# One slot of the K matmuls moved ahead of the last convolution chunk of the first bundle

## The chip, the cores and the metric

The kernel runs on one core of a Trainium2 chip. The metric is the device time of one execution in microseconds; the median over runs is compared. Engines are named as in the profile: PE multiplies matrices (PEld loads its weights), DVE and ACT work element by element, POOL and SP mostly issue DMAs. Each engine takes its own instructions in the order in which the program gives them, and waits on semaphores for the others.

## What is computed

The input x has 8 batches of 4160 rows and 192 columns. A causal convolution of 7 taps comes first; its taps are a softmax of `weight`, one set for each of 8 heads of 24 columns. Its output, called y here, goes into a channel mix:

```python
x_prev = np.concatenate([np.zeros((B, 1, D)), x[:, :-1, :]], axis=1)   # x is y, the convolution's output
xk = mu_k * x + (1.0 - mu_k) * x_prev
xr = mu_r * x + (1.0 - mu_r) * x_prev
k = np.maximum(xk @ w_k, 0.0)          # 192 -> 1024
v = k * k @ w_v                        # 1024 -> 192
r = 1.0 / (1.0 + np.exp(-(xr @ w_r)))  # 192 -> 192
return r * v
```

The kernel multiplies in bf16 and adds up in fp32.

## The kernel before

**Tiling.** Batches go in pairs; the two batches of a pair lie in the two halves of the 128 partitions, and the 192 columns in three chunks of 64 (`NC` = 3). y is kept transposed (`yT`, columns on partitions, time along the row). Time is cut into steps of 512 rows; the first step and two others have 256. A step of L rows has L*8/512 slots: a slot is one PSUM tile of 128 by 1024 fp32 that holds a part of the K product (`k_mm`, L592), read by one ReLU on ACT (`k_relu`, L604) and squared by one DVE instruction (`k_square`, L618). The first step has slots 0 to 3, the second 4 to 11. Four slots make a bundle, and the bundles are run in order; the last loop of the file calls one function for each.

**A first-step slot.** `k_mm` of a slot of the first step issues 12 matmuls of 64 by 256: three column chunks, two blocks of 128 output columns, and the two halves of the partitions, which alternate. So the first matmul of a slot reads the weights `wk` in partitions 0 to 63 and the second those in partitions 64 to 127.

**The order is written by hand.** The whole program is emitted under a manual schedule: each engine gets its instructions in the order of the calls. PSUM tiles come from a ring of four, given out in turn, so a tile is reused by the fourth allocation after it, once its readers are done.

**Before the bundles.** `prologue()` issues the loads. K's weights are loaded in four DMAs by POOL (`load_wk`, L225): output columns 0 to 511 for partitions 0 to 63, the same for 64 to 127, then columns 512 to 1023 likewise. Slots 0 and 1 need the first two, slots 2 and 3 the others. PE runs matmuls on zeros in the meantime.

**Bundle one** (`bundle_first`) makes y for the first two groups of rows (3 and 4 blocks of 120 rows) straight in transposed form. There are six chunks, one for each group and each 64 columns. `conv_t` (L412) issues 24 matmuls for a chunk of the first group and 32 for one of the second, and `to_yT` (L422) copies the result from PSUM to `yT` on ACT. For the first group DVE then forms the difference of neighbours (`diff`, L535) and xk (`mix`, L548). After the loop, DVE forms the second step's difference and xk, the first column chunk ahead and the other two later (`diff`, L535; `scale`, L566; `add_y`, L572): `diff(1, slice(1, 3))` needs the copies of the fifth and sixth chunk. PE goes on with slots 0 to 3. The four squares are at the end of the bundle, after the second step's xk in DVE's order.

**Bundle two** (`bundle_second`) has slots 4 to 7, which read the second step's xk, between the three chunks of the third group. The first two of these are copied by DVE (L422), the third by ACT. Bundles three and four use `bundle_third` and `bundle_rest`; there PE also transposes y of a group (`tr`, L501, copied by DVE at L510), and convolves later groups in another form (L318, L392). A one-element memset on DVE (`x_tile`, L124) stands ahead of the x loads of each later group, and POOL's load waits for it.

Of the kernel before, what the change touches and what calls it, by code (L numbers as in the profile page):

```python
# [14 lines left out]
def kernel(  # L15
# [47 lines left out]
    for p in range(NPAIR):  # L63
# [5 lines left out]
        for L in sizes:  # L69
            ns = L * NF // STEP  # L70
# [8 lines left out]
    n = 0  # L79
# [102 lines left out]
    n = groups[0][2] * 2 * D  # L182
# [97 lines left out]
    def turn_mu():  # L280
        nc.tensor.transpose(out=warm_ps[:, 1, 0 : 2 * NC], in_=mu_raw, identity=ident6)
# [120 lines left out]
    def conv_t(g, c, o, blocks):  # L402

        for n, i in enumerate(blocks):
            for first_piece in (True, False):
                for s in range(2):
                    for q in range(2):
                        c0 = c * Q + q * 32
                        lo, hi = c0 // G, (c0 + 31) // G
                        h, m = (hi, 32) if first_piece else (lo, hi * G - c0)  # L410
                        p0 = s * Q + q * 32
                        nc.tensor.matmul(  # L412
                            out=o[p0 : p0 + m, n * BLK : (n + 1) * BLK],
                            lhsT=xbs[g][:, i, s, c0 : c0 + m],
                            rhs=toe[:, h, 0:BLK],
                            start=True,
                            stop=True,
                        )

    def to_yT(g, c, o, b0, b1, copy):  # L420
        c0 = YC + groups[g][1] + b0 * BLK
        copy(out=yTs[0][:, c, c0 : c0 + (b1 - b0) * BLK], in_=o[:, 0 : (b1 - b0) * BLK])  # L422
# [28 lines left out]
    def new_yT(p):  # L451
        yTs[p] = two.tile([P, 3, -(-(YC + S) // 16) * 16], BF16, tag="yT", name="yT")
        y_drams[p] = dram.tile([NROW, 2 * D], BF16, tag=f"y{p % 2}", name="y_dram")
        nc.vector.memset(yTs[p][:, :, 0:YC], 0.0)
# [76 lines left out]
    def diff(s, cs=slice(0, 3)):  # L531
        L = steps[s][2]
        if cs.start == 0:
            diffs[s] = three.tile([P, 3, STEP], BF16, tag="diff", name="d")
        nc.vector.tensor_tensor(  # L535
            out=shaped(s, diffs[s][:, cs, :L]), in0=y_of(s, cs, 1), in1=y_of(s, cs, 0), op=ALU.subtract
        )

    def mix(s, i, sl=slice(0, NC)):

        L = steps[s][2]
        d = diffs[s]
        if s == 0 and i == 0:
            if sl.start == 0:
                xks[s] = two.tile([P, NC, STEP], BF16, tag="xk", name="xk")
            t = xks[s]
            c = sl.start
            nc.vector.scalar_tensor_tensor(  # L548
                out=t[:, c, :L],
                in0=d[:, c, :L],  # L550
                scalar=mu[:, i, c : c + 1],
                in1=y_of(s, sl, 0)[:, 0, :],
                op0=ALU.mult,
                op1=ALU.add,
            )
            return
        scale(s, i, *range(sl.start, sl.stop))
        add_y(s, i, sl)

    def scale(s, i, *cs):  # L560
        L = steps[s][2]
        if s not in (xks, xrs)[i]:
            (xks, xrs)[i][s] = (two, three)[i].tile([P, NC, STEP], BF16, tag=("xk", "xr")[i], name=("xk", "xr")[i])
        t = (xks, xrs)[i][s]
        for c in cs:
            nc.vector.tensor_scalar(  # L566
                out=t[:, c, :L], in0=diffs[s][:, c, :L], scalar1=mu[:, i, c : c + 1], scalar2=None, op0=ALU.mult
            )

    def add_y(s, i, sl=slice(0, NC)):  # L570
        o = shaped(s, (xks, xrs)[i][s][:, sl, : steps[s][2]])
        nc.vector.tensor_tensor(out=o, in0=o, in1=y_of(s, sl, 0), op=ALU.add)  # L572
# [3 lines left out]
    def k_mm(n, cs=range(NC)):  # L576


        s, j = slots[n]
        L = steps[s][2]  # L580
        xk = xks[s]
        if cs[0] == 0 and n not in k_ps:
            k_ps[n] = ring.tile([P, 2, BANK], FP32, tag="k", name="ps_k")
        ps = k_ps[n]
        nf = STEP // L

        for c in cs:
            for f in range(nf):
                fs = slice((j * nf + f) * P, (j * nf + f + 1) * P)
                for i in range(2):  # L590
                    r = slice(i * Q, (i + 1) * Q)
                    nc.tensor.matmul(  # L592
                        out=ps[:, i, f * L : (f + 1) * L],
                        lhsT=wk[r, c, fs],
                        rhs=xk[r, c, :L],
                        start=c == 0 and f == 0,
                        stop=c == NC - 1 and f == nf - 1,
                    )

    def k_relu(n):  # L600
        ps = k_ps.pop(n)
        k_sb = four.tile([P, 2 * STEP], BF16, tag="k_sb", name="k_sb")
        k_sbs[n] = k_sb
        nc.scalar.activation(out=k_sb, in_=ps.rearrange("p a b -> p (a b)"), func=AF.Relu)  # L604

    def k_square(n):
        s, j = slots[n]
        L = steps[s][2]
        k_sb = k_sbs.pop(n)
        if j == 0:  # L610
            k2s[s] = three.tile([P, NF, 2 * STEP], BF16, tag="k2", name="k2")
        nf = STEP // L
        i = k_sb
        o = k2s[s][:, j, :]
        if nf > 1:
            i = k_sb.rearrange("p (b f t) -> p f b t", b=2, f=nf)
            o = k2s[s][:, j * nf : (j + 1) * nf, 0 : 2 * L].rearrange("p f (b t) -> p f b t", b=2)
        nc.vector.tensor_tensor(out=o, in0=i, in1=i, op=ALU.mult)  # L618
# [198 lines left out]
    def run(table, b, part=slice(None)):  # L817
        for fn, a in table.get(b, [])[part]:
            fn(*a)
# [50 lines left out]
    def bundle_first(ns):  # L870
        new_yT(0)
        tiles = [ring.tile([P, 2, BANK], FP32, tag="k", name="ps_t") for _ in range(2)]
        for n, (g, c) in enumerate((g, c) for g in range(2) for c in range(NC)):
            o = tiles[n % 2][:, n // 2 % 2, :]
            conv_t(g, c, o, range(groups[g][2]))
            if n == 0:
                turn_mu()
            to_yT(g, c, o, 0, groups[g][2], nc.scalar.copy)
            if g == 0:
                diff(0, slice(c, c + 1))  # L880
                if c == 0:
                    nc.vector.tensor_copy(out=mu.rearrange("p i c -> p (i c)"), in_=warm_ps[:, 1, 0 : 2 * NC])
                mix(0, 0, slice(c, c + 1))

        diff(1, slice(0, 1))
        mix(1, 0, slice(0, 1))
        for n in ns[:2]:
            k_mm(n)
            k_relu(n)
        diff(1, slice(1, 3))  # L890
        scale(1, 0, 1, 2)
        add_y(1, 0, slice(1, 3))
        for n in ns[2:]:
            k_mm(n)
            k_relu(n)
        for n in ns:
            k_square(n)
        run(late, 0)
# [111 lines left out]
    with tc.manual_schedule():  # L1010
        prologue()
        for b in range(-20, 0):
            for table in (early, rq, rs, xt, mix_a, mix_b, mix_c, vq, late):
                assert b not in table, b
        for b in range(quads[-1][2] + 1):
            run(early, b)
            if b == 0:
                bundle_first(bundles[b])
            elif b == 1:
                bundle_second(b, bundles[b])  # L1020
            elif b == 2:
                bundle_third(b, bundles[b])
            elif b < len(bundles):
                bundle_rest(b, bundles[b])
            else:
                if b == len(bundles):
                    k_square(bundles[-1][3])
                    v_out(*vq[b - 1][0])
                run(rq, b)
                run(rs, b)  # L1030
                for q in vq.get(b, ()):
                    v(*q)
                    v_out(*q)
                run(late, b)
# [30 lines left out]
```

## Time and profile before

| what | us |
|---|---|
| median of 3 runs (411.14 to 412.48) | 412.45 |
| the profiled execution | 411.14 |
| its span, first to last instruction | 409.4 |
| PE busy | 401.5 (98%) |
| DVE busy | 371.3 (91%) |
| ACT busy | 354.6 (87%) |
| mean granted clock of PE | 1.000 |

The span is the time between the first and the last instruction on the core; the rest of the profiled execution's time lies around it. Busy times of different engines overlap. A timeline line gives start and length in us, engine, source line, operation, output and inputs, the shape, how many instructions were merged into the line, and in brackets the idle time before it with the event that ended it. A merged line's length runs from the first start to the last end. Matmuls are pipelined: one starts before the one ahead of it has ended, and their ends are modelled.

### The profile page before, as it was taken

Reading aid. Unit: us, or ns where it says so; the run is one execution under the profiler, and the core shown is the slowest. Engines: PE = TensorE matmul, PEld = TensorE weight load, DVE = VectorE, ACT = ScalarE, POOL = GpSimd, SP = SyncE. Lnnn points to the kernel's source line nnn. Section 1 sums busy time; section 2 is a strip of 40 time slices with the busy share of each in tenths; the row PEclk is TensorE's granted clock in tenths of the full one; section 3 lists DMA queues with packets and bytes.
Section 4 is the critical chain, followed back from the end, with each engine's and each line's share of the span. In section 5 each row is a group of like instructions: output and inputs, shape, how many; then the busy total and the mean of one; then the engine's idle time right before and its main releaser. Section 6 shows DMA issues by size and latency. Waiting matters only on the chain.

```text
span 409.4 us, 17415 instructions
## 1 busy us (share of the span) xinstructions
PE 401.5 (98%) x7670; PEld 303.8 (74%) x7670; DVE 371.3 (91%) x672; ACT 354.6 (87%) x426; POOL 57.7 (14%) x91
## 2 busy tenths in 40 slices
PE   7999999999999999999999999999999999999996
PEld 4667767767867777777877777777777778777795
DVE  5999899998989999989999998999999899999973
ACT  5999988898998889998898998889899878877781
POOL 8622022030060004104020022000000000000000
PEclk9999999999999999999999999999999999999999
DMA  9999989996779988989995998977523756221223
GB/s 148 191 200 202 190 186 215 244 199 189 152 105 221 257 176 125 226 231 169 197 151 152 227 176 123 171 196 187 132 78 90 199 143 159 79 72 48 78 80 117
DMA packets 139123, 66.35 MB, mean 162 GB/s; under 512 B 89364, under 2 KB 139048, under 8 KB 139048
## 3 DMA queue, kind: packets, MB, share of 16 engines
q1 hardware_dynamic: 95704, 48.32, 47.6%
q0 software_dynamic: 42544, 16.36, 34.4%
q8 instruction: 60, 0.98, 1.0%
q10 hardware_dynamic: 800, 0.57, 0.5%
q14 instruction: 15, 0.12, 0.1%
HBM read 33.29 MB, written 36.99 MB: 172 GB/s over the span
## 4 chain that ended last, share of the span: by engine, by line
PE 93%; DMA 3%; DVE 2%; issue 0%; ACT 0%; ACTq 0%; DVEq 0%
PE ps_v L680 41%; PE ps_k L592 39%; PE ps_r L649 8%; PE ps_c L363 2%; DMA xb<-in_x_dram 2%; PE ps_v L632 1%; PE ps_t L412 1%; DMA x_f<-in_x_dram 1%; PE ps_c L318 1%; DVE k L618 1%; DVE yT L422 0%; ACT yT L422 0%; DVE o_sb L696 0%; DVE xk L566 0%; DVE d L535 0%
## 5 line engine op out<-in xcount | busy, mean ns | idle before, releaser
L604 ACT ACTIVATE k_sb<-ps_k 128x1024 bf16<-128x1024 f32 x260 | 253.4, 1040 | 32.9 <-PE ps_k L592 32.2
L618 DVE TENSOR_TENSOR k<-k_sb 128x1024 bf16<-128x1024 bf16 x260 | 173.2, 686 | 24.8 <-ACT k_sb L604 24.5
L592 PE MATMUL ps_k<-xk,wk 64*128 64x512 bf16 (+1 forms) x1632 | 191.7, 367 | 0.8 <-DMA wk<-in_moe_w_k_dram 0.5
L680 PE MATMUL ps_v<-wv,k 64*128 64x192 bf16 x4032 | 188.6, 243 | 0.1
L680 PEld LDWEIGHTS <-k 64*128 64x128 bf16 x4032 | 168.7, 94 | 12.4 <-issue 4.7
L592 PEld LDWEIGHTS <-wk 64*128 64x128 bf16 x1632 | 84.2, 94 | 55.0 <-issue 1.0
L153 POOL DMA_DIRECT2D xb<-in_x_dram x62 | 43.7, 714 | 142.3 <-DVE xb L124 58.1
L696 DVE TENSOR_TENSOR o_sb<-ps_v,r_sb 128x768 f32<-128x768 f32 x64 | 60.8, 949 | 2.6 <-issue 2.4
L660 ACT ACTIVATE r_sb<-ps_r 128x768 bf16<-128x768 f32 x65 | 53.7, 828 | 9.2 <-PE ps_v L680 7.6
L336 ACT CAST y<-ps_c 128x960 bf16<-128x960 f32 (+2 forms) x84 | 52.6, 709 | 0.0
L649 PEld LDWEIGHTS <-xr 64*128 64x128 bf16 x780 | 34.8, 94 | 14.5 <-issue 0.7
L649 PE MATMUL ps_r<-wr,xr 64*128 64x192 bf16 x780 | 43.4, 243 | 0.1
L566 DVE TENSOR_SCALAR xr<-d,mu 128x512 bf16<-128x512 bf16 (+1 forms) x102 | 35.7, 354 | 0.0
L535 DVE TENSOR_TENSOR d<-yT 128x1536 bf16<-128x1536 bf16 (+4 forms) x36 | 31.2, 866 | 2.0 <-ACT yT L422 2.0
L566 DVE TENSOR_SCALAR xk<-d,mu 128x512 bf16<-128x512 bf16 (+1 forms) x99 | 32.8, 360 | 0.1
L572 DVE TENSOR_TENSOR xr<-xr,yT 128x1536 bf16<-128x1536 bf16 (+1 forms) x33 | 31.1, 941 | 1.1
L572 DVE TENSOR_TENSOR xk<-xk,yT 128x1536 bf16<-128x1536 bf16 (+3 forms) x33 | 30.4, 923 | 0.1
L519 POOL COPY y_tail<-yT 128x195 bf16<-128x195 bf16 x4 | 3.1, 774 | 89.7 <-DMA yT<-y_dram 89.7
L363 PEld LDWEIGHTS <-toe 32*32 32x32 bf16 x640 | 4.4, 87 | 8.6 <-issue 7.4
L363 PE MATMUL ps_c<-xb,toe 32*32 32x240 bf16 x640 | 9.3, 267 | 0.0
L126 POOL MEMSET xb<- 32x384 bf16 x3 | 1.2, 408 | 55.5 <-DVE xb L124 48.6
L412 PEld LDWEIGHTS <-xb 128*32 128x32 bf16 (+3 forms) x264 | 5.1, 116 | 3.0 <-ACT xb L246 1.7
(58 smaller groups left out, 65.7 us busy)
## 6 DMA issues: line engine op xcount, KB each, us to landing
out_dram<-o_sb SPq DMA_DIRECT2D x128, 192.0 KB
xb<-in_x_dram POOLq DMA_DIRECT2D x52, 240.0 KB, 8.5
y_dram<-y SPq DMA_DIRECT2D x40, 195.0 KB
y_dram<-y SPq DMA_DIRECT2D x16, 210.0 KB
xb<-in_x_dram POOLq DMA_DIRECT2D x4, 228.0 KB, 5.0
xb<-in_x_dram POOLq DMA_DIRECT2D x4, 192.0 KB, 7.0
wk<-in_moe_w_k_dram POOLq DMA_DIRECT2D x4, 192.0 KB, 6.5
xb<-in_x_dram POOLq DMA_DIRECT2D x2, 216.0 KB, 5.0
```

The source lines that it names most:

```text
L153: nc.gpsimd.dma_start(out=xb[q0 : q0 + rows, lo:hi, s, :], in_=bass.AP(tensor=x.tensor, offset=x.offset + (b * S + t0 + lo * step) * D, ap ...
L336: nc.scalar.copy(out=bass.AP(tensor=y.tensor, offset=y.offset + d, ap=[y.ap[0], [m * 2 * D, 2], [2 * D, m], [Q, 2], [1, b - a]],), in_=bas ...
L535: nc.vector.tensor_tensor(out=shaped(s, diffs[s][:, cs, :L]), in0=y_of(s, cs, 1), in1=y_of(s, cs, 0), op=ALU.subtract)
L566: nc.vector.tensor_scalar(out=t[:, c, :L], in0=diffs[s][:, c, :L], scalar1=mu[:, i, c : c + 1], scalar2=None, op0=ALU.mult)
L572: nc.vector.tensor_tensor(out=o, in0=o, in1=y_of(s, sl, 0), op=ALU.add)
L592: nc.tensor.matmul(out=ps[:, i, f * L : (f + 1) * L], lhsT=wk[r, c, fs], rhs=xk[r, c, :L], start=c == 0 and f == 0, stop=c == NC - 1 and f ...
L604: nc.scalar.activation(out=k_sb, in_=ps.rearrange("p a b -> p (a b)"), func=AF.Relu)
L618: nc.vector.tensor_tensor(out=o, in0=i, in1=i, op=ALU.mult)
L649: nc.tensor.matmul(out=ps[:, i, k * D : (k + 1) * D], lhsT=xr[q, c, ts], rhs=wr[q, c, :], start=c == 0, stop=c == NC - 1,)
L660: nc.scalar.activation(out=r_sbs[s, j], in_=r_ps.pop((s, j))[:, :, 0 : 2 * D], func=AF.Sigmoid)
L680: nc.tensor.matmul(out=v_ps[s, j][:, bank, k * D : (k + 1) * D], lhsT=k2s[s][q, f, t * P : (t + 1) * P], rhs=wv[q, f, :], start=half == 0 ...
L696: nc.vector.tensor_tensor(out=o_sb.rearrange("p (b t) d -> p b (t d)", b=2), in0=v_ps.pop((s, j)), in1=r_sbs.pop((s, j)), op=ALU.mult,)
```

## The change

Slot 0 of the first step (its 12 matmuls and its ReLU) is emitted inside the loop over the six chunks, before the sixth (`n == 5`), in place of after the loop. Slot 1 stays where it was. Nothing else is touched.

```diff
@@ in bundle_first
         for n, (g, c) in enumerate((g, c) for g in range(2) for c in range(NC)):
             o = tiles[n % 2][:, n // 2 % 2, :]
+            if n == 5:
+                k_mm(ns[0])
+                k_relu(ns[0])
             conv_t(g, c, o, range(groups[g][2]))
             if n == 0:
                 turn_mu()
...
         diff(1, slice(0, 1))
         mix(1, 0, slice(0, 1))
-        for n in ns[:2]:
-            k_mm(n)
-            k_relu(n)
+        k_mm(ns[1])
+        k_relu(ns[1])
         diff(1, slice(1, 3))
         scale(1, 0, 1, 2)
         add_y(1, 0, slice(1, 3))
```

On PE the 12 matmuls of slot 0 now stand ahead of the 32 matmuls of the sixth chunk, and on ACT slot 0's ReLU stands ahead of the sixth chunk's copy. The order on DVE, POOL and SP is the same, and so is the order in which PSUM tiles are given out.

## The prediction

> **What bounds the kernel now.** I read the page's busy table first (PE 98% of the span, DVE 91%, ACT 87%), then the table of stretches, to see which engine has no room at which time.
>
> ```profile
> core 0: us, PE busy (x) PEld busy (x) DVE busy (x) ACT busy (x) POOL busy (x), PEclk, DMA share, GB/s
> 16.00:20.30 4.30, 4.07 (x126) 2.63 (x124) 4.26 (x12) 4.15 (x5) 2.80 (x5) 1.00 1.59 192
> 20.30:29.70 9.40, 8.95 (x147) 6.22 (x141) 9.33 (x19) 9.08 (x12) 1.75 (x4) 1.00 1.58 193
> 29.70:45.70 16.00, 15.95 (x290) 11.49 (x291) 15.80 (x28) 15.32 (x21) 4.04 (x6) 1.00 1.12 201
> 45.70:100.00 54.30, 54.30 (x980) 40.22 (x980) 49.74 (x91) 49.27 (x61) 8.85 (x13) 1.00 1.10 214
> 100.00:400.00 300.00, 299.85 (x5749) 229.15 (x5746) 278.59 (x492) 264.26 (x313) 27.27 (x41) 1.00 0.74 150
> ```
>
> From 29.7 us on PE has 0.2 us of idle time in 370 us: a start that is late by x ends late by x. From 16 to 29.7 us it is DVE that has no room (13.59 of 13.70 us busy), while PE has 0.68 us. The edit lies before that, at 10 to 14 us, so the question is what DVE gets there and when. The chain of waits, in order of time, gives it (start, us, what):
>
> ```profile
> 8.91 1.80 PE ps_t L412 x41
> 10.73 1.08 ACT yT L422 x2
> 11.84 0.71 DVE d L535
> 12.57 0.94 DVE xk L566 x2
> 13.53 0.69 DVE xk L572
> 14.22 2.50 DVE k L618 x4
> 16.72 1.13 DVE yT L422 x2
> ```
>
> The last two of bundle one's six convolution chunks are copied by ACT (10.73, 11.25), and the moment the sixth copy ends DVE starts the difference for the second step; from 11.84 on DVE is never free. The chain later passes through a load of x (18.77 to 26.67), but DVE goes on working beside that load, so I follow DVE, not the load. The timelines of PE (first five lines; the last is the place where PE next waits for DVE) and ACT (two lines), then the issue of K's weights and the landing of their second piece (asked for alone):
>
> ```profile
> 7.24 3.96 PE L412 MATMUL ps_t<-toe,xb 128*32 128x120 bf16 x144
> 11.13 1.60 PE L592 MATMUL ps_k<-xk,wk 64*128 64x256 bf16 x25
> 13.19 2.78 PE L592 MATMUL ps_k<-xk,wk 64*128 64x256 bf16 x35 [0.46 <-DMA wk<-in_moe_w_k_dram]
> 17.71 0.60 PE L412 MATMUL ps_t<-toe,xb 128*32 128x120 bf16 x32
> 29.75 0.82 PE L592 MATMUL ps_k<-xk,wk 64*128 64x512 bf16 x6 [0.26 <-DVE yT L510]
> ...
> 10.73 1.07 ACT L422 CAST yT<-ps_t 128x480 bf16<-128x480 f32 x2 [0.24 <-PE ps_t L412]
> 12.11 6.74 ACT L604 ACTIVATE k_sb<-ps_k 128x1024 bf16<-128x1024 f32 x7 [0.30 <-PE ps_k L592]
> ...
> 4.20 2.55 POOL L225 DMA_DIRECT2D wk<-in_moe_w_k_dram x4
> L225 POOL DMA_DIRECT2D wk<-in_moe_w_k_dram x1: 640/640/640, 4.9 to 4.9; - x1
> DMA to landing us min/median/max: 6.3/6.3/6.3
> ```
>
> Two things to see. The second piece of K's first half (rows 64 to 127, needed by every second matmul of slot 0) is issued at 4.9 us and lands 6.3 us later, at 11.2; slot 0's matmuls begin at 11.13. So in the old order the sixth chunk filled PE while these weights were on their way. And ACT's seven ReLUs stand 0.95 us apart ((6.74-1.02)/6, one taking 1.02), the two copies 0.52 apart (one 0.56).
>
> **The change part by part.** Nothing is added or taken away; on PE 12 matmuls and their weight loads (slot 0) pass ahead of the 32 of chunk six, on ACT slot 0's ReLU passes ahead of the copy of chunk six. DVE's, POOL's and SP's orders stay. Slot 0's xk is done on DVE at 10.11 (9.63+0.48) and its output buffer was read last at 8.0, so neither holds it.
>
> 1. PE reaches slot 0 earlier. Chunk five's copy starts at 10.73 after waiting for PE, and a matmul there takes about 0.3 us from start to end, so its last one starts near 10.4. Slot 0's first matmul can run then; the second waits for the weights of 11.2. PE stalls about 0.8 us, and queued behind it are chunk six and slot 1, which need nothing of these weights' second piece or have it later.
> 2. Slot 0 itself then runs as before, from 11.24 for 12 x 0.055 = 0.66 us of issue (25 take 1.60 less the 0.27 tail of the last, so 0.055 each), and its ReLU starts at 12.11 as before. The move brings this ReLU nothing.
> 3. Chunk six follows at about 12.0 and takes 0.60 (the row of 32 such matmuls at 17.71): done at 12.6 instead of 11.2.
> 4. Its copy now stands behind slot 0's ReLU on ACT: it starts one ReLU spacing after 12.11, at 13.06, and ends at 13.62; before, 11.80 (10.73+1.07). That is +1.8. ACT's 0.30 wait before slot 0's ReLU grows to 0.8, since the copy that stood in it is gone.
> 5. DVE's difference of the second step goes from 11.84 to about 13.65. Queued behind it in program order are the scaling and adding (done 14.22, then 16.0), the four squares, the casts of the third group and all of bundles two and three. Nothing of DVE's can pass. The idle time that could take some of it back is 0.03 us from 13.2 to 16 and 0.11 from 16 to 29.7: 0.14.
> 6. On PE the wait of 0.46 for the second half of K's weights goes (PE gets there at about 13.2, where the old wait ended), but slots 4 and 5 now wait for the second step's xk, from about 14.5 to 16.0. This is not a second cost: PE needs DVE again at 29.75, and that wait is the later one.
> 7. DMA: the x loads tied to DVE's tiny memset at 18.39 are issued 1.7 later. Their issue-to-landing of 8 to 9 us is queueing behind other loads, and their users in bundle four run at 39 us against landings to 31: hidden, with 7 us to spare.
>
> Sum: 1.81 - 0.14 = 1.7 us at 29.75 us, and no room after it. The profiled execution took 411.14 (409.4 of span, 1.7 around it): 412.8. It is the shortest of the three shown; on the median of 412.45 the same step gives 414.15.
>
> Bounds of the one unknown, when the weights land: the four pieces' times to landing run from 6.0 to 7.0 us, so 10.9 to 11.9 for this one. With 10.9 the copy would end 0.3 earlier: +1.4. With 11.9 the ReLU would start at 12.8 and the copy end at 14.3: +2.4, of which the old order would itself pay up to 0.6, since there too the ReLUs would run later into squares that have no room. I take 11.2, as measured, and keep +1.4 to +2.4.
>
> **The clock against the row.** PE's matmul rate steps up just at the place of the edit. The same 128x120 matmuls, first from 6.3 to 10.3 us and then from 10.72 to 11.0:
>
> ```profile
> L412 PE MATMUL ps_t<-toe,xb 128*32 128x120 bf16 x68 | 3.9, 302 | 0.8 <-ACT xb L246 0.8
> L412 PE MATMUL ps_t<-toe,xb 128*32 128x120 bf16 x16 | 0.6, 231 | 0.0
> ```
>
> A chunk of 32 took 0.80 to 0.82 us of the timeline before this step (start to start of two copies: 9.93 to 10.73) and 0.60 with its tail after. The profile's granted clock reads 1.00 all through, so it does not show the step; only the durations do. In the sum I take the step where the trace has it. [...]
>
> **The rivals.**
>
> *A, the other side: the fast rate comes late, and it is slower beyond the bound.* If PE goes on at its slow rate through slot 0 and chunk six, slot 0 takes 302/231 to 0.80/0.44 times as long (0.44 is the 0.60 less a tail of about 0.16 hidden under the next matmul), up to 1.2 us instead of 0.66, and the chunk 0.80. The ReLU starts at 12.65, chunk six ends near 13.6, its copy at 14.2: +2.4 to +2.5, and squares behind late ReLUs may add some tenths. That is 414.9 to 415.2. For it: the stall comes at 10.4, the step at about 10.6. Against: PE had idle gaps in the stretch before and stepped up all the same. It decides where the step moves past about 11.2.
>
> *B, the delay is partly taken up.* Two of the three times shown are 1.3 us above the profiled one. If that excess is a wait of DVE's between 11.84 and 29.7 (ReLUs that come later when PE is slow), the new delay eats it first: 1.7 - 1.3 = 0.4, so 412.9; from an excess of 1.7 on, no change at all, 412.45. For it: the squares follow the ReLUs closely (the fourth ReLU ends at 15.99, its square starts at 16.03). Against: the excess may as well lie ahead of the edit, in the first loads, and then it simply adds.
>
> *C, it does what it says and helps.* If K's weights were there by 10.4, slot 0's ReLU would fill ACT right after the copy of chunk five and ACT's 0.30 us wait would go: -0.3, 412.15. But the copy of chunk six would still stand a ReLU later, 0.95 us on DVE, so this needs DVE to have 1 us of room, which the table of stretches excludes; with the weights alone it is +0.95, 413.4.
>
> **How the numbers follow.** The main case (DVE late by about 1.7, all of it kept) has 0.55: 414.1, with 413.6 to 414.7 as its own range. A has 0.27, B 0.14, C 0.04. A measurement of this kernel tells about 0.5%, 2.06 us, from no change; so slower means above 414.51. The main case gives a quarter of itself to that (0.13), A three quarters (0.20): 0.33 slower. Faster, below 410.39, needs a gain that no row offers: 0.03. The rest, 0.64, is within. The range leaves out a tenth on each side: below 412.6 lies the full form of B, above 415.2 the end of A.
>
> **What the new profile should show.** On PE, one or two matmuls of slot 0 near 10.45, a wait of 0.7 to 0.8 us for the DMA of wk, the rest at 11.24, then 32 matmuls of chunk six, and a wait of about 1.5 us at 14.5 that ends with DVE's xk. On ACT, an idle time of 0.8 ahead of the first ReLU (still 12.1), then the copy at 13.06 to 13.62. On DVE, 1.8 us idle before the difference at 13.65, and none up to about 31. PE's wait for DVE's copy of the transposes at about 31.45. I am wrong if DVE shows idle time between 14 and 31 in either kernel's usual run, if the weights land much off 11.2, or if chunk six takes 0.8 instead of 0.6.

## The result and the profile after

The changed kernel takes 413.30 us (median of 22 runs, 411.99 to 415.94) against 412.12 for the kernel before (22 runs, 410.46 to 412.71). The ratio is 1.0040, with a 95% interval from 1.0027 to 1.0053: 1.65 us longer (0.0040 x 412.12), between 1.1 and 2.2. That is inside the 0.5% that the prediction took as its bound for "no change", though clear of zero with this many runs. The means of the same runs, 413.50 and 411.86, lie 1.64 apart; the plain difference of the two medians is only 1.18.

The page's head of the changed kernel; the busy times of DVE and ACT are as before, PE's is 1.4 us higher, and the span is longer:

```profile
span 412.0 us, 17415 instructions
PE 402.9 (98%) x7670; PEld 303.9 (74%) x7670; DVE 371.1 (90%) x672; ACT 354.5 (86%) x426; POOL 57.6 (14%) x91
```

The profiled execution took 413.72, 2.58 more than that of before (411.14). Its chain of waits, in order of time from 8 to 32 us (start, us, what):

```profile
4.88 6.57 DMA wk<-in_moe_w_k_dram
11.45 0.05 issue
11.50 0.84 PE ps_k L592 x11
12.36 1.02 ACT k_sb L604
13.38 0.48 ACT yT L422
13.88 0.70 DVE d L535
...
31.57 0.60 PE ps_k L592 x3
```

Before, this chain came from the convolution chunks through two copies to DVE at 11.84. Now it starts at the second DMA of K's weights (issued 4.88, landed 11.45), goes through slot 0's matmuls and its ReLU, and only then to the sixth copy and DVE, at 13.88. The timeline of PE and of ACT shows the places:

```profile
10.20 0.28 PE L592 MATMUL ps_k<-xk,wk 64*128 64x256 bf16 x1 [0.77 <-DMA wk<-in_moe_w_k_dram]
11.50 0.82 PE L592 MATMUL ps_k<-xk,wk 64*128 64x256 bf16 x11 [1.02 <-DMA wk<-in_moe_w_k_dram]
12.25 0.99 PE L412 MATMUL ps_t<-toe,xb 128*32 128x120 bf16 x32
13.18 4.61 PE L592 MATMUL ps_k<-xk,wk 64*128 64x256 bf16 x48
...
31.57 0.60 PE L592 MATMUL ps_k<-xk,wk 64*128 64x512 bf16 x4 [0.27 <-DVE yT L510]
...
13.29 0.56 ACT L422 CAST yT<-ps_t 128x480 bf16<-128x480 f32 x1
14.68 1.02 ACT L604 ACTIVATE k_sb<-ps_k 128x1024 bf16<-128x1024 f32 x1 [0.83 <-PE ps_k L592]
```

PE runs one matmul of slot 0, waits twice for the weights (0.77 and 1.02 us), and chunk six stands behind. The sixth copy begins at 13.29 instead of 11.25. PE's wait for DVE's copy of the transposes has moved from 29.75 to 31.57: +1.82. So 1.82 of the 2.58 us between the two profiled executions are there by 31.6 us. The remaining 0.76 come later. About half of it is in two waits of PE between 100 and 400 us, where the list of the kernel before has none,

```profile
PE ps_r L649 <- issue: 0.2, 1, 0.2
PE ps_v L680 <- issue: 0.2, 1, 0.2
```

and, as said under the last heading, such waits come and go from run to run. The rest lies in no wait that the list shows.

One more thing is new, the matmul rate. The table of stretches:

```profile
core 0: us, PE busy (x) PEld busy (x) DVE busy (x) ACT busy (x) POOL busy (x), PEclk, DMA share, GB/s
8.75:12.20 3.45, 1.66 (x60) 1.10 (x48) 2.03 (x6) 1.02 (x2) 2.63 (x4) 1.00 1.18 168
12.20:15.60 3.40, 3.40 (x59) 2.48 (x58) 1.65 (x4) 2.41 (x3) 2.16 (x4) 0.50 1.57 191
```

After a stretch in which PE was busy for 1.66 of 3.45 us, the granted clock is 0.50 for 3.4 us; chunk six takes 0.99 there instead of 0.60, and 48 matmuls of slots take 4.61 us. In this execution the rate had already stepped up near 8.75 (128x120 matmuls took 300 ns from 6.7 to 8.6 us and 230 after 8.8), and it fell again after the stretch with the stall. That the drop goes with the stall is borne out by the single runs, below under the fillers.

### The profile page after: what moved, and what is told of

Read it like the earlier page. It is cut to its first block, busy times and chain, and to the rows that moved or that the text cites. A ratio compares the mean times of both kernels' runs of the same rounds, so it can differ in the third digit from the quotient of the medians.

```text
span 412.0 us, 17415 instructions
## 1 busy us (share of the span) xinstructions
PE 402.9 (98%) x7670; PEld 303.9 (74%) x7670; DVE 371.1 (90%) x672; ACT 354.5 (86%) x426; POOL 57.6 (14%) x91
## 4 chain that ended last, share of the span: by engine, by line
PE 92%; DVE 4%; DMA 2%; POOL 1%; issue 1%; ACT 1%; POOLq 0%; DVEq 0%; ACTq 0%
PE ps_v L680 41%; PE ps_k L592 39%; PE ps_r L649 8%; PE ps_c L363 2%; DMA wk<-in_moe_w_k_dram 2%; DVE k L618 1%; PE ps_v L632 1%; PE ps_c L318 1%; POOL xb L153 0%; ACT k_sb L604 0%; DVE xk L572 0%; DVE d L535 0%; DVE xr L566 0%; DVE xk L566 0%; DVE yT L422 0%
```

## The experiments

Two theories. The first is the prediction's: the end is set by the moment at which DVE gets the sixth chunk's copy, and DVE and then PE keep the delay. The second is its rival A, widened by what the profile shows: the stall of PE and the slow rate after it cost the time. Each experiment ran with the kernel before on the same chip (12 runs against 23 or 35).

### ACT's half alone

```diff
 (against the kernel before, in the loop over the chunks; after the loop only slot 1 is left, as in the change)
             conv_t(g, c, o, range(groups[g][2]))
+            if n == 5:
+                k_mm(ns[0])
+                k_relu(ns[0])
...
             to_yT(g, c, o, 0, groups[g][2], nc.scalar.copy)
```

> ACT's half of the change alone: on PE chunk six stays ahead of slot 0, as before, and only slot 0's ReLU stands ahead of the copy of chunk six on ACT. Theory 1 (what counts is when DVE gets the sixth copy, and DVE keeps every tenth): the ReLU starts at 12.1 as before, the copy at 13.06 instead of 11.25, DVE's second difference 1.8 us later than before: +1.6 to +1.8 us on the time before, as much as the whole change. Theory 2 (the stall of PE and the slow matmul rate after it are what costs): PE does not stall ahead of chunk six here, so the rate stays up and the time is at most 0.5 us above before.

Measured: 412.92 us, ratio 1.0030 [1.0011, 1.0049], +1.2 us (0.5 to 2.0). Timeline of ACT, DVE and PE:

```profile
12.71 1.02 ACT L604 ACTIVATE k_sb<-ps_k 128x1024 bf16<-128x1024 f32 x1 [1.68 <-PE ps_k L592]
13.63 0.55 ACT L422 CAST yT<-ps_t 128x480 bf16<-128x480 f32 x1
14.21 0.69 DVE L535 TENSOR_TENSOR d<-yT 128x1024 bf16<-128x1024 bf16 x1 [2.67 <-ACT yT L422]
31.95 0.60 PE L592 MATMUL ps_k<-xk,wk 64*128 64x512 bf16 x4 [0.37 <-DVE yT L510]
```

PE does not stall ahead of chunk six here, its order is that of the kernel before, and the time is still longer by about what the whole change costs in these tests (less than the expected 1.6 to 1.8, which the interval takes in). A copy that stands behind a ReLU is enough. (The rate was low in this execution without any stall ahead of it: 50 slot matmuls from 11.2 took 3.97 us, and the ReLU came at 12.71, not at 12.1. So a low rate at this place is not the change's alone.)

### PE's half alone

```diff
 (against the changed kernel)
             if n == 5:
                 k_mm(ns[0])
-                k_relu(ns[0])
             conv_t(g, c, o, range(groups[g][2]))
...
             to_yT(g, c, o, 0, groups[g][2], nc.scalar.copy)
+            if n == 5:
+                k_relu(ns[0])
```

> PE's half of the change alone: slot 0's matmuls ahead of chunk six on PE, the copy of chunk six ahead of slot 0's ReLU on ACT. Theory 1: the copy follows chunk six, which ends at 12.6 (13.2 at the slow rate), so DVE's difference starts at about 13.2 to 13.8: +1.3 to +1.9 us. Theory 2: the same stall and rate as in the whole change, so the same time as the changed kernel, +1.2 to +1.7. If ACT's order alone were the cause, this would be at most +0.3.

Measured: 413.03 us, ratio 1.0028 [1.0009, 1.0046], +1.2 us (0.4 to 1.9).

```profile
11.48 1.46 PE L592 MATMUL ps_k<-xk,wk 64*128 64x256 bf16 x11 [0.56 <-DMA wk<-in_moe_w_k_dram]
12.87 0.99 PE L412 MATMUL ps_t<-toe,xb 128*32 128x120 bf16 x32
13.92 0.56 ACT L422 CAST yT<-ps_t 128x480 bf16<-128x480 f32 x1 [3.52 <-PE ps_t L412]
14.51 0.70 DVE L535 TENSOR_TENSOR d<-yT 128x1024 bf16<-128x1024 bf16 x1 [3.60 <-ACT yT L422]
32.03 0.39 PE L592 MATMUL ps_k<-xk,wk 64*128 64x512 bf16 x2 [0.37 <-DVE yT L510]
```

Here the copy waits for PE, not for the ReLU. The rate was low in this execution, which adds to the wait: 11 matmuls of slot 0 took 1.46 us, against 0.82 in the changed kernel, and chunk six took 0.99. By the times each half alone costs about as much as the other. By the lines the two do not add: in the whole change the copy waits for whichever is later.

### DVE's delay without the move

```diff
 (against the kernel before)
-        diff(1, slice(1, 3))
+        for _ in range(3):
+            diff(1, slice(1, 3))
```

> The kernel before, with the second step's difference of column chunks two and three formed three times instead of once: two more DVE instructions of 0.69 us each at the very place where the change makes DVE late, nothing else moved. Theory 1: DVE has no room from there to 29.7 us and PE none after it: +1.2 to +1.4 us, all of it kept. The rival that part of a delay is taken up: +0.4 us or less.

Measured: 412.84 us, ratio 1.0025 [1.0007, 1.0043], +1.0 us (0.3 to 1.8).

```profile
11.98 2.15 DVE L535 TENSOR_TENSOR d<-yT 128x1024 bf16<-128x1024 bf16 x3 [0.20 <-ACT yT L422]
30.96 0.82 PE L592 MATMUL ps_k<-xk,wk 64*128 64x512 bf16 x6 [0.37 <-DVE yT L510]
```

The difference ends at 14.13 instead of 12.53, and PE goes on at 30.96 instead of 29.75 (+1.21). But these +1.21 are not all DVE's. The orders of PE and ACT are those of the kernel before, and in this execution the matmul rate was low (50 slot matmuls from 11.28 took 3.96 us, where 25 took 1.60 before), so the ReLUs were late as well:

```profile
12.94 4.69 ACT L604 ACTIVATE k_sb<-ps_k 128x1024 bf16<-128x1024 f32 x5 [0.99 <-PE ps_k L592]
```

The first began at 12.94 instead of 12.11, and the fourth ended at 16.70 instead of 15.99. An estimate from these rows: without the added differences the fourth square would have had to wait for that ReLU, until about 16.7. With them it began at 17.24. So in this execution only about 0.5 of the added 1.46 us arrived, and the late ReLUs account for the other 0.7 of the 1.21. Over the runs the added 1.46 us cost 1.0 (0.3 to 1.8): a delay of DVE alone does arrive at the end, but that all of it does is not shown.

### Slot 0's weights earlier

```diff
 (against the changed kernel, in prologue)
-        load_wk(0, DF // 2)
+        load_wk(0, DF // 4)
+        load_wk(DF // 4, DF // 2)
```

> The changed kernel, with K's first half loaded as two quarters (two more DMAs of 96 KB, in place of two of 192 KB four of 96), so that slot 0's weights are there about 1 us earlier, near 10.2. Theory 1: PE's stall goes, slot 0's ReLU starts near 11.3, the sixth copy ends near 12.8: DVE 1.0 us late, +0.8 to +1.0 us on the time before, 0.7 below the changed kernel. Theory 2: with the stall gone the cost is gone: +0.3 or less. If the weights' landing has no part in it: as the changed kernel.

Measured: 412.23 us, ratio 1.0019 [0.9997, 1.0041], +0.8 us (-0.1 to 1.7).

```profile
10.00 1.25 PE L592 MATMUL ps_k<-xk,wk 64*128 64x256 bf16 x12
11.30 1.02 ACT L604 ACTIVATE k_sb<-ps_k 128x1024 bf16<-128x1024 f32 x1 [0.62 <-PE ps_k L592]
12.22 0.55 ACT L422 CAST yT<-ps_t 128x480 bf16<-128x480 f32 x1
12.81 0.70 DVE L535 TENSOR_TENSOR d<-yT 128x1024 bf16<-128x1024 bf16 x1 [1.40 <-ACT yT L422]
30.43 0.82 PE L592 MATMUL ps_k<-xk,wk 64*128 64x512 bf16 x6 [0.37 <-DVE yT L510]
```

The stall is gone, the ReLU starts at 11.30, and the difference at 12.81 instead of 13.88, where theory 1 put it (12.8). The time is where theory 1 put it too, but its interval is too wide to tell this from no change. What the lines show is that even with the weights there, the ReLU ahead of the copy leaves DVE 1 us late. (The quartered load has a price of its own: PE waits 0.98 us for the second half of K's weights, until 13.64.)

### PE kept busy in the stall, beside the changed kernel itself

```diff
 (against the changed kernel)
             if n == 5:
+                for _ in range(4):
+                    nc.tensor.matmul(out=w_ps[:, 1, :], lhsT=ones_t, rhs=zeros, start=True, stop=True)
                 k_mm(ns[0])
```

> The changed kernel with four matmuls of zeros (128x512 each, no result used) on PE between chunk five and slot 0, where it otherwise waits for K's weights: 0.9 us of PE work at the fast rate, 1.7 at the slow one. Theory 1 (DVE's start of the second difference decides, by slot 0's ReLU and the copy behind it): the same as the changed kernel within 0.3 us where the rate is up, or up to 0.6 longer where the fillers run slowly and reach past the landing of the weights. Theory 2 (the stall lets the matmul rate drop, and that costs): the rate stays up, chunk six and slots 1 to 3 run fast, 0.5 to 1.0 us below the changed kernel.

> The changed kernel itself, beside the others on the same chip: +1.2 to +2.0 us on the time before.

Measured, on one chip: with the fillers 413.41 us, ratio 1.0032 [1.0015, 1.0049], +1.3 us (0.6 to 2.0); the changed kernel 413.02, ratio 1.0027 [1.0004, 1.0050], +1.1 us (0.2 to 2.1), just under the 1.2 expected. The fillers first, then the changed kernel:

```profile
9.79 1.04 PE L877 MATMUL w_ps<-zeros,ones_t 128*128 128x512 bf16 x4
12.03 0.60 PE L412 MATMUL ps_t<-toe,xb 128*32 128x120 bf16 x32
13.05 0.55 ACT L422 CAST yT<-ps_t 128x480 bf16<-128x480 f32 x1
13.64 0.69 DVE L535 TENSOR_TENSOR d<-yT 128x1024 bf16<-128x1024 bf16 x1 [2.13 <-ACT yT L422]
```

```profile
12.16 0.60 PE L412 MATMUL ps_t<-toe,xb 128*32 128x120 bf16 x32
13.78 0.69 DVE L535 TENSOR_TENSOR d<-yT 128x1024 bf16<-128x1024 bf16 x1 [2.28 <-ACT yT L422]
31.29 0.82 PE L592 MATMUL ps_k<-xk,wk 64*128 64x512 bf16 x6 [0.36 <-DVE yT L510]
```

With the rate up at chunk six (0.60 us), the kernel gains nothing. In the second profile of the changed kernel it was up there too (0.60 us), and the difference came at 13.78, against 13.88 where the rate had dropped. The reason is in the first profile of the changed kernel: chunk six, slow, ended at 13.24, and the ReLU ahead of its copy held ACT up to then anyway.

The granted clock of every single run says how often the rate drops. The profiled execution with the drop has a mean clock of 0.995. Values of 0.994 to 0.996 stand in 5 of the 34 runs of the changed kernel and in 3 of the 12 of PE's half, which has the same stall, and in 1 of the 12 with earlier weights; in none of the 36 of ACT's half, of the kernel with two more differences and of the fillers, and in none of the 93 of the kernel before that ran beside the experiments. So the drop goes with the stall, but it is not what makes the kernel longer: the 19 runs without it among the first 22 have a median of 413.22, against 413.30 for all. Theory 2 falls as far as the drop goes: it is real, and other work covers it. In the profiles of ACT's half and of the two more differences a rate that has not yet stepped up does not show in this clock (1.00 throughout, with 50 slot matmuls from 11.2 us on in 3.97 and 3.96), so these counts say nothing of that.

### Less work for DVE in the kernel before

```diff
 (against the kernel before)
         if s == 0:
-            at(mix_a, 1, mix, s, 1)
             continue
...
         run(late, 0)          # end of bundle one
+        xrs[0] = three.tile([P, NC, STEP], BF16, tag="xr", name="xr")
+        for c in range(NC):
+            nc.gpsimd.tensor_scalar(
+                out=xrs[0][:, c, : steps[0][2]], in0=diffs[0][:, c, : steps[0][2]],
+                scalar1=mu[:, 1, c : c + 1], scalar2=None, op0=ALU.mult,
+            )
+        o = xrs[0][:, :, : steps[0][2]]
+        nc.gpsimd.tensor_tensor(out=o, in0=o, in1=y_of(0, slice(0, NC), 0), op=ALU.add)
```

> The kernel before, with the first step's xr (three scalings of 128x256 and one addition of 128x768, 1.3 us of DVE's chain between 18.4 and 19.6) moved to POOL, behind its load of the fifth group's x. Theory 1 (DVE is the engine without room from 11.8 to 29.7): DVE is 1.3 us earlier at 29.7, PE's two waits there of 0.42 us go, and PE's own work sets the time: -0.3 to -0.5 us. If DVE were not what PE waits for: no change. If POOL is too late for the r matmuls (21.5) or slows DVE by working beside it: up to +1 us.

Measured: 415.47 us, ratio 1.0071 [1.0048, 1.0094], +2.9 us: a miss.

```profile
17.98 4.98 POOL L900 TENSOR_SCALAR xr<-d,mu 128x256 bf16<-128x256 bf16 x3
24.82 0.67 PE L649 MATMUL ps_r<-wr,xr 64*128 64x192 bf16 x12 [3.02 <-POOL xr L908]
```

The scaling that DVE did in 0.28 us takes POOL 1.66, and the first r matmuls wait 3.0 us for it. It does not test DVE as meant. It does show two other things.

The first is a stall whose drop is not covered. After the wait the rate drops (the mean granted clock of this execution is 0.996, against 1.000 in that of before), and

```profile
25.32 2.71 PE L680 MATMUL ps_v<-wv,k 64*128 64x192 bf16 x32
```

takes 2.71 us instead of 1.50. The profiled execution is 4.9 us longer than that of before, not 3.0. The five runs whose clock is 1.000 took 412.99 to 414.62, the seven with less 415.34 to 417.81: the runs with the drop are about 2 us longer, and the median of 2.9 is a mixture of the two.

The second is the kernel before itself: up to 18 us this program is unchanged. DVE's timeline:

```profile
10.79 0.69 DVE L535 TENSOR_TENSOR d<-yT 128x1024 bf16<-128x1024 bf16 x1
13.20 0.69 DVE L618 TENSOR_TENSOR k<-k_sb 128x1024 bf16<-128x1024 bf16 x1 [0.22 <-ACT k_sb L604]
14.12 0.69 DVE L618 TENSOR_TENSOR k<-k_sb 128x1024 bf16<-128x1024 bf16 x1 [0.23 <-ACT k_sb L604]
15.18 0.69 DVE L618 TENSOR_TENSOR k<-k_sb 128x1024 bf16<-128x1024 bf16 x1 [0.37 <-ACT k_sb L604]
16.09 0.69 DVE L618 TENSOR_TENSOR k<-k_sb 128x1024 bf16<-128x1024 bf16 x1 [0.22 <-ACT k_sb L604]
16.70 0.65 DVE L422 CAST yT<-ps_t 128x480 bf16<-128x480 f32 x1
```

The difference began at 10.79, 1.05 us earlier than in the profiled kernel before, and DVE then waited 1.04 us for the four ReLUs, so the casts behind the squares began at 16.70, against 16.63 there. In the old order an earlier difference is no gain.

### Attempts at a better version of the kernel before

```diff
 (matmuls of zeros ahead of the convolution; then also the quartered load, and that load alone)
-    WARM = (3, 2)
+    WARM = (4, 3)
...
-        load_wk(0, DF // 2)
+        load_wk(0, DF // 4)
+        load_wk(DF // 4, DF // 2)
```

> The kernel before, with two more matmuls of zeros ahead of the first convolution chunk (one in each of the two idle stretches of PE, 3.7 to 4.2 and 5.6 to 6.3 us), to bring the fast matmul rate earlier. If the late rate delays the sixth copy in the usual run: -0.2 to -0.5 us. If chunk four's wait for its x and DVE's own work set the sixth copy anyway: no change; if the added matmuls reach past the landing of x: up to +0.3.

> The kernel before, with the two added matmuls of zeros and with K's first half loaded as quarters. In the run with the added matmuls alone DVE's second difference was early (11.47), yet DVE then waited 1.0 us for the ReLUs, which start with the landing of slot 0's weights at 11.2. If the sixth copy and the ReLUs are two bounds of nearly the same height in the kernel before, then only both edits together lower them: slot 0's ReLU near 11.4, DVE's difference near 11.2, DVE 0.5 to 0.7 us earlier at 29 us, -0.5 to -0.8 us on the time before. If DVE alone bounds: as with the added matmuls alone, -0.1 to -0.5.

> The kernel before, with K's first half loaded as quarters only. Slot 0 stands behind chunk six, which ends at 11.2 in any case, so the ReLUs come 0.1 to 0.2 us earlier and DVE's difference stays at 11.8: no change within 0.3 us.

Measured: the added matmuls alone 411.66 us, 0.9987 [0.9968, 1.0006]; both 412.32, 1.0005 [0.9982, 1.0027]; the load alone 412.21, 1.0007 [0.9984, 1.0029]. None is told from the kernel before, and the expected gain of both together did not come, so no version that beats it was found. DVE's timeline with the matmuls alone, then with the load alone, shows what holds a better start back:

```profile
11.47 0.70 DVE L535 TENSOR_TENSOR d<-yT 128x1024 bf16<-128x1024 bf16 x1 [0.37 <-ACT yT L422]
15.22 0.69 DVE L618 TENSOR_TENSOR k<-k_sb 128x1024 bf16<-128x1024 bf16 x1 [0.43 <-ACT k_sb L604]
16.14 0.69 DVE L618 TENSOR_TENSOR k<-k_sb 128x1024 bf16<-128x1024 bf16 x1 [0.22 <-ACT k_sb L604]
```

```profile
11.57 0.69 DVE L535 TENSOR_TENSOR d<-yT 128x1024 bf16<-128x1024 bf16 x1
15.92 0.69 DVE L618 TENSOR_TENSOR k<-k_sb 128x1024 bf16<-128x1024 bf16 x1 [0.99 <-ACT k_sb L604]
```

Where the difference comes before 11.6, in these two and in POOL's experiment, DVE waits for the ReLUs at its squares instead. With the quartered load these are late for a reason of its own: the second half of K's weights let PE go on at 14.00, against 13.19 before. In the old order the copies and the ReLUs are two bounds of nearly one height; in the two profiles of the new order the copy alone bounds.

## Why the prediction was right, point by point

The forecast was 414.1 us, or +1.7 on a median before of 412.45. Measured were 413.30 against 412.12: +1.65 by the ratio, +1.18 by the medians. The mechanism is the one forecast; the size is at or below what was forecast, and part of the agreement is luck, as the errors named below cancel. The table follows DVE's second difference through the kernels, by their profiled executions (us; its end is its start plus length):

| kernel | difference ends | PE goes on after DVE's copy | between |
|---|---|---|---|
| before | 12.53 | 29.75 | 17.2 |
| changed | 14.57 | 31.57 | 17.0 |
| changed, second profile | 14.47 | 31.29 | 16.8 |
| ACT's half | 14.90 | 31.95 | 17.0 |
| PE's half | 15.21 | 32.03 | 16.8 |
| two more differences | 14.13 | 30.96 | 16.8 |
| weights earlier | 13.51 | 30.43 | 16.9 |
| fillers | 14.33 | 31.31 | 17.0 |

Over eight executions and 2.7 us of differing starts the distance stays within 0.4 us. This is the claim that carried the forecast, that DVE keeps the delay, and for differences that begin at 11.8 or later these lines bear it out, with the reservation made above about late ReLUs where the rate is low. Three more profiles of the old order are not in the table: with both edits of the better start the distance is 17.3 (difference from 12.12 on), and with the added matmuls and the load alone, where the difference begins before 11.6 and DVE then waits for ReLUs, it is 17.7 and 18.1.

- Step 1, PE's stall: right in kind, too small in the first profile. Two waits of 0.77 and 1.02 against 0.8 predicted. The rate had stepped up early, so PE was there sooner, and also waited for the weights' first piece, which the working left out. In the second profile it was one wait, of 0.53.
- Step 2, slot 0's ReLU as before at 12.1: 12.36 and 12.27 in the two profiles. The weights landed at 11.4, not 11.2, within the bounds given.
- Steps 3 to 5: chunk six at 12.25 and 12.16 (predicted 12.0), the copy at 13.29 and 13.19 (13.06), the difference at 13.88 and 13.78 (13.65): +2.0 and +1.9 instead of +1.8. Chunk six took 0.99 us in the first profile, which the prediction named as a sign of being wrong, and 0.60 in the second; it made no difference, since slot 0's ReLU ended later than the slow chunk.
- Step 6: in the second profile slots 4 and 5 wait 0.76 us for DVE's xk, half of the predicted 1.5, and in the first not at all, since PE was behind by itself. As argued there, this does not set the end.
- The room given back was put at 0.14 us; by the table it is 0.2 to 0.4 (17.2 against 16.8 to 17.0). With the later landing this makes +1.82 and +1.54 at the place where PE goes on, around the 1.7 of the sum: a start that was put too early and too little given back nearly cancel.
- Rival A, a rate that steps up late, was not met in either profile of the changed kernel; the first had a drop in its place, after slot 0 had run fast (11 matmuls in 0.82 us; the granted clock is 1.00 up to 12.2, 0.50 from 12.3 to 15.6 and 1.00 from 15.7), and slot 0's ReLU hid the slow chunk. That a stall ahead of the step makes it late is not shown: in ACT's half the rate was low from 11.2 us on (50 slot matmuls in 3.97) with no stall ahead. PE's half shows A's case: slow slot 0, slow chunk, the difference at 14.51, 2.67 after that of before, where A said 2.4 to 2.5. How often the changed kernel runs so is not known. The fillers showed no gain from keeping the rate.
- Rival B is not excluded, and one of the prediction's signs of being wrong, DVE idle after 14 us, is there: in POOL's experiment, which is the kernel before up to 18 us, DVE waited 1.04 us at squares, and in two profiles of the old order with small edits 0.65 and 1.2, where the changed kernel waits 0.09 us or not at all. In the first of these the wait only made up for an early difference. In executions with a low rate, as in the profile with two more differences, the ReLUs are late by themselves, and by the estimate made there about 0.9 of 1.46 us of a delay is taken up. If such executions are frequent, that fits medians 1.2 to 1.3 apart where the traces have 1.5 to 1.8. How frequent they are, no run shows.
- Rival C: earlier weights did not turn the change into a gain. DVE's difference was 0.97 us late, as C's second half said (0.95); by the ratios the earlier weights took a third to a half of the added time away, though the interval does not settle how much.

## What to carry to other kernels

Before moving a block of work ahead to fill an engine sooner, look up when its own operands land, and what stands behind it on every in-order queue: here a slot that could hardly start earlier held back a copy that another engine was waiting for, on PE and on ACT, and either alone was enough (+1.2 us each). Follow the engine without room, not the busiest one: PE was 98% busy, but DVE between 12 and 30 us decided. A delay counts from the later of two bounds: where the squares would have waited for ReLUs anyway, the first part of it costs nothing (by the estimate above, 0.9 of 1.46 us in the profile with two more differences). And whether a stall's drop of the matmul rate costs anything depends on what stands behind the slow matmuls: here a ReLU hid them, while behind POOL's late scaling they cost about 2 us.

## What the runs showed that was not expected

- POOL took 1.66 us (1.42 to 1.86) for a scaling of 128x256 in bf16 that takes DVE 0.28, and 1.71 for the addition of 128x768 that DVE does in 0.56. While POOL worked, one of six squares on DVE took 2.04 us instead of 0.68.
- The granted clock read 1.00 in all stretches before the first step up of the rate, though chunks ran at the low rate (300 ns for a matmul that takes 230 later), and 0.50 after a step down. In these profiles it shows a drop, not a start at the low rate.
- Between 100 and 400 us PE stands without a recorded reason in some profiles: twice 0.2 us in the changed kernel (near 245 and 253 us), 0.5 in ACT's half and with two more differences, 1.0 in the changed kernel again, 1.0 and 0.5 with the load alone; not at all in the kernel before and with the added matmuls alone. It does not follow the edits, but is as large as the effect measured, so single executions of these kernels can't be compared by their spans. Its cause stays open.
